# Moving VectorE's extra operations behind the last output of a gate/up unit

## The chip, the cores and the metric

The kernel runs on one core of one Trainium2 chip. A core has a matrix engine (TensorE, PE in the profile, with its weight loads as PEld), three elementwise engines (VectorE or DVE, ScalarE or ACT, GpSimd or POOL) and SyncE (SP), which issues most of the transfers. The engines run side by side, each through its own list of instructions in order, and wait for one another through semaphores. The metric is the device time of one execution in microseconds; lower is better.

## The reference

The inputs are in bfloat16: x of 2048 tokens by 1024, the attention weights, the gate, up and down weights (1024 x 3584 twice, 3584 x 1024 once), and a conditioning row c.

```python
mod = (silu(c) @ w_mod)                      # six rows of 1024: sa, ca, ga, sb, cb, gb
h = layernorm(x) * (1 + ca) + sa
x = x + ga * A(h)                            # 32 heads of linear attention, then @ wo
h = layernorm(x) * (1 + cb) + sb
x = x + gb * ((gelu(h @ w_gate) * (h @ w_up)) @ w_down)
```

The change touches the last line alone, and the scaling of h ahead of it.

## The kernel before, in words

**Stages.** From 0 to about 242 us the kernel does the modulation rows, the first layer norm, the attention and most of its output projection. From there to 605 us it does the gate and up products, and from 605 us to the end the down product with the last addition to x. TensorE's list has no barrier between stages.

**Gate/up units.** The 2048 tokens are two halves p of 1024. For each half the 3584 hidden columns are 14 pairs of 128, so there are 28 units v = 0 to 27 (`unit(v)`). A unit needs, for gate and up (t = 0 and 1), a 256 x 1024 by 1024 x 1024 product. It is done as a 2 x 2 x 2 block product with seven block products in place of eight, P1 to P7, each four matmuls deep over the contraction, so 8 matmuls with both t and 56 in a unit. They are run in the order 1, 5, 6, 2, 7, 3, 4. From 5 on but for 2, the two t alternate from matmul to matmul; in P1 and P2 t = 0 is done before t = 1. The seven products need sums of blocks as operands:

- `t_sum(v, k)` (L1438, VectorE, two operations of 128 x 512 each, tiles tp) makes the weight sums of unit v; k = 3 is a copy on ScalarE (L1427). There is one set of tp tiles, so the sums of unit v + 1 follow the product of unit v that last read the tile. P5 reads tp 0, P6 tp 1, P7 tp 2, P3 tp 3, P4 tp 4.
- `s_sum(p, i, j)` (L1418, 128 x 1024, tiles ss) makes the sums of the normalised tokens, once for each half. `ar_copy(p)` (L1404, ScalarE) copies a block of tokens into another type, as two operations.
- `mod2` (L754, VectorE) and `mod2_act` (L785, ScalarE) scale and shift the normalised tokens of the second half before that.

Results stand in eight PSUM banks, four pairs BA, BB, BC, BE (one of a pair for gate, one for up). P1 writes BA. `pcp` (L1470, ScalarE) copies BA to BB, for t = 0 and then 1; P6 adds to BB. P5 writes BE, `escp` (L1473, ScalarE) copies it to es. After P6 `padd` (L1476, VectorE) writes BB + es to BC, for both t, and P7 adds to BB after that; then `padd` writes BB + es to BE. P2, P7, P3 and P4 each end one of a unit's four outputs, in BA, BE, BC and BB: `gelu` (L1481, ScalarE) reads the gate bank, `y_out` (L1485, VectorE) multiplies with the up bank into yr. The last one, of P4 in BB, is put off: `held` keeps it until P1's first half of the next unit has been recorded, and then `y_store(v)` (L1493, SP) sends the unit's yr to scr_y. So pcp of a unit, which writes BB, waits for the y_out of the unit before.

**The order around it.** In these two stages nothing is planned by costs: the order of each engine's list is the order in which the Python code records operations. `unit` records each product and behind it the operations that belong to it, and then runs the hooks that were hung on it: `hook(v, k, fn)` runs fn behind product k of unit v, after that product's own work. So a hook on (v, 4) comes behind the unit's last product and ahead of the next unit's P1, and with it ahead of the held y_out; a hook on (v + 1, 1) comes behind that y_out, behind pcp and behind `t_sum(v + 1, 4)`. Before, the extra work of VectorE is hung in turn on (v, 7) and (v, 4): mod2 in units 5 and 6 (and 9), s_sum of the second half in units 10 to 13, and from unit 14 on the weight sums of the down stage.

**Down stage.** Step j takes 256 tokens and 1024 output columns over 28 blocks of hidden columns in 14 pairs k. It has the same seven products over most pairs (`dprod`, L1611): over pairs 0 to 12 in steps 1 to 7, over pairs 0 to 5 (NEA = 6) in step 0, where the other pairs are done plainly (`plain`). `raw_load(k)` (L1565, SP) loads the weights of a pair (tiles bx and wst), `b_sum(k, i)` makes their five derived operands (L1577 on VectorE; i = 3 is a copy on ScalarE, L1571), `y_load` (L1586, SP) fetches yl, and `a_sum(i, ..)` (L1605, VectorE) makes the sums of yl. `b_sums` yields four calls per pair, the last with i = 3 and 4 together. `ew` is that row for pairs 0 to 7, spent by hooks in units 14 to 27; `lw` is the rest, and `lws(n)` spends n calls of it. `dpcp` (L1644), `descp` (L1648) and `dpadd` (L1652, VectorE) do what pcp, escp and padd do above.

Of the kernel before, what the change touches and what calls it, by code (L numbers as in the profile page):

```python
# [346 lines left out]
def bass_adaLN_cond__linear_attn_block__geglu_ffn__prompt_kernel(  # L347
# [18 lines left out]
    with ExitStack() as es:  # L366
# [410 lines left out]
        def mod2(p, h, c0, n, dc0=0, dc1=NDC):  # L777
            mods(h2ap, r_h2p, (p, h), sc2, c0 * P, (c0 + n) * P, dc0, dc1, "h2")
# [620 lines left out]
        S32 = [[t_.ap().bitcast(f32) for t_ in r_] for r_ in SS]  # L1399
        T32 = [t_.ap().bitcast(f32) for t_ in TP]  # L1400

        def ar_copy(p):
            for k in (0, 2):
                sch.op(A, lambda e, k=k: e.activation(A22R[p][:, k:k + 2, :], H2[p][1][:, ND2 + k:ND2 + k + 2, :], ACTF.Copy),  # L1404
                       rd=r_h2(p, 1, ND2 + k, ND2 + k + 2), wr=r_ar(p, k, k + 2), note=f"arcp {p}.{k}")

# [16 lines left out]
        def t_sum(u, k):  # L1423
            if k == 3:
                ap, rd = wq(u, 1, 1)
                for t in range(2):
                    sch.op(A, lambda e, t=t: e.activation(TP[3][:, t, :, :], ap[:, t, :, :], ACTF.Copy), rd=rd[t:t + 1], wr=r_tp(3, t, t + 1), note=f"brcp u{u}")  # L1427
                return
            if k == 0:
                (in0, r0), (in1, r1) = wq(u, 0, 1), wq(u, 0, 0)  # L1430
            elif k == 1:
                (in0, r0), (in1, r1) = wq(u, 1, 1), (T32[0], r_tp(0))
            elif k == 2:
                (in0, r0), (in1, r1) = wq(u, 1, 1), wq(u, 0, 1)
            else:
                (in0, r0), (in1, r1) = wq(u, 1, 0), (T32[1], r_tp(1))
            for t in range(2):
                sch.op(V, lambda e, t=t: e.tensor_tensor(TP[k][:, t, :, :], in0[:, t, :, :], in1[:, t, :, :], ALU.subtract),  # L1438
                       rd=r0[t:t + 1] + (r1[t:t + 1] if len(r1) == 2 else [(r1[0][0] + t * 2048, r1[0][0] + (t + 1) * 2048, r1[0][2])]),
                       wr=r_tp(k, t, t + 1), note=f"tsum{k} u{u}")  # L1440
# [58 lines left out]
        def hook(v, k, fn):  # L1499
            HK.setdefault((v, k), []).append(fn)  # L1500

        def unit(v, order=(1, 5, 6, 2, 7, 3, 4)):
            more = v + 1 < 2 * NFP
            for k in order:
                if isinstance(k, tuple):
                    wo_chunk(*k)
                    continue
                if callable(k):
                    k()
                    continue  # L1510
                late = v == 0 and k == 2
                gb_, gk, yl, yh = (None, 1, 0, 0) if late else {2: (BA, 0, 0, 0), 7: (BE, 1, 1, 1), 3: (BC, 0, 1, 0), 4: (BB, 0, 0, 1)}.get(k, (None, 1, 0, 0))
                if k > 2:
                    for dc in range(ND2):
                        for t in range(2):
                            prod(v, t, k, [dc])
                for t in range(2):
                    if k < 3:
                        prod(v, t, k)
                    if k == 1:  # L1520
                        if held[0]:
                            held[0]()
                            held[0] = None
                            y_store(v - 1)
                        pcp(t)
                    elif k == 5:
                        escp(t)
                    elif k == 6:
                        padd(t, BC)
                    elif k == 7:  # L1530
                        padd(t, BE)
                    if gb_ is not None and t == gk:
                        gelu(gb_)
                        ig = (gi[0] - 1) % 2
                if k == 2 and v + 2 < 2 * NFP:
                    wt_dma(v + 2)
                if k == 4:
                    held[0] = lambda: y_out(ig, BB, v, 0, 1)
                elif gb_ is not None:
                    y_out(ig, gb_, v, yl, yh)  # L1540
                if k == 1:
                    if v == 0:
                        ar_copy(0)
                    else:
                        t_sum(v, 4)
                if more:
                    if k == (3 if v == 0 else 5):
                        t_sum(v + 1, 0)
                    if k == (3 if v == 0 else 2):
                        t_sum(v + 1, 1)  # L1550
                    if k == 3:
                        t_sum(v + 1, 3)
                        t_sum(v + 1, 2)
                for f_ in HK.pop((v, k), ()):
                    f_()

# [62 lines left out]
        def dprod(j, i, k0, k1, n=512):  # L1619
            t, ks = j % 2, range(k0, k1)  # L1620
            if i in (1, 2):
                lhs = [ya(i - 1, 0, k) for k in ks]
                rhs = [(BXT[k][:, i - 1, :], r_bx(k, i - 1, i)) for k in ks]
            else:
                xi, ti = {5: (0, 0), 6: (1, 1), 7: (0, 2), 3: (1, 3), 4: (2, 4)}[i]
                lhs = [(XS[xi][:, k, :], r_xq(xi, k, k + 1)) for k in ks]
                rhs = [(TT[k][ti][:, 0:n], r_bt(k, ti)) for k in ks]
            b = {1: BA, 2: BA, 5: BE, 6: BB, 7: BB, 4: BB, 3: BC}[i] + t
            dmm(b, i in (1, 5) and k0 == 0, lhs, rhs, f"down j{j} P{i}", 0, n)
# [83 lines left out]
        for i in range(4):  # L1713
            hook(i + 1, 2, lambda i=i: x1_store(i))
        for n in range(4):
            hook(5 + n // 2, (7, 4)[n % 2], lambda n=n: mod2(1, 0, 0, 4, 2 * n, 2 * n + 2))
        hook(9, 7, lambda: mod2(1, 1, 0, 4, 0, 3))
        hook(9, 4, lambda: mod2(1, 1, 0, 4, 3, 5))
        hook(9, 6, lambda: mod2_act(1, 1, 0, 4, 5, 6))
        hook(9, 3, lambda: mod2_act(1, 1, 0, 4, 6, 8))  # L1720
        hook(10, 3, lambda: ar_copy(1))
        for n in range(8):
            i, j = divmod(n, 2)
            hook(10 + n // 2, (7, 4)[n % 2], lambda i=i, j=j: s_sum(1, i, j))
        hook(12, 2, lambda: raw_load(0))
        hook(13, 2, lambda: raw_load(1))
        ew = b_sums(range(NEA + 2))
        for n in range(4 * NEA):
            v, k = 14 + n // 2, (7, 4)[n % 2]
            hook(v, k, lambda: next(ew)())  # L1730
            if n % 4 == 3 and 2 + n // 4 < NEA:
                hook(v, k, lambda n=n: raw_load(2 + n // 4))
# [3 lines left out]
        hook(24, 2, lambda: raw_load(6))  # L1736
        hook(26, 2, lambda: raw_load(7))
        hook(26, 7, lambda: next(ew)())
        hook(26, 4, lambda: next(ew)())
        V_ = 2 * NFP - 1  # L1740
        hook(V_, 5, lambda: a_sum(0, 0, NEA))
        hook(V_, 5, lambda: next(ew)())
# [14 lines left out]
        def lws(n):  # L1757
            for _ in range(n):
                next(lw)()
# [10 lines left out]
        dprod(0, 5, 0, NEA)  # L1770
        descp(0)
        a_sum(2, 0, NEA)
        lws(3)
        dprod(0, 6, 0, NEA)
        dpadd(0, BC)
        a_sum(3, 0, NEA)
        dprod(0, 2, 0, NEA)
        for l in range(2):
            y_load(1, l, 0, NEA)
# [1 line left out]
        dpadd(0, BE)  # L1781
        dprod(0, 3, 0, NEA)
        dprod(0, 4, 0, NEA)
        lws(6)
        for k in range(NEA, NKP):
            for s_ in range(2):
                for c in range(2):
# [148 lines left out]
```

## Time and profile before

| | us |
|---|---|
| median of three runs (790.52, 791.15, 792.69) | 791.15 |
| the profiled execution, its own time | 790.65 |
| its span, first to last instruction | 788.8 |
| TensorE busy in it | 775.3 |
| VectorE busy | 636.1 |
| ScalarE busy | 342.5 |
| clock granted to TensorE | 1.0 throughout |

A row of the timeline has start and length in us, engine, line, operation, tiles written and read, shapes and count; where the engine sat idle before it, the idle time and what ended it stand in brackets. In a list of waits the numbers are the total in us, how many times, and the longest. A row of the table of windows gives the window's length and then, for each engine, busy time and instructions. A unit starts where TensorE's rows turn to the tiles h20a (first half) or h21a (second half) and wt after a row with ar; unit 1 starts at 262.01, unit 14 at 428.18, the down stage at 605.01. A few matmul records are missing in the trace, so a group of eight can show as seven.

### The profile page before, as it was taken

The page shows a single profiled execution, that of the slowest core. Times are in us where ns is not written, and L with a number is a line of the kernel's source. Part 1 is how long each engine was busy: PE and PEld are TensorE (multiplying, and loading weights), DVE is VectorE, ACT ScalarE, POOL GpSimd, SP SyncE. Part 2 cuts the span into 40 slices and gives each one's busy share as a digit, 9 for nine tenths or more (in the row PEclk, how much of TensorE's full clock was granted, in tenths as well). Part 3 has the DMA queues.
Part 4 walks back from the last instruction along what each step waited for, and adds up shares of the span by engine and source line. Part 5 has one row for each costly group of instructions (what it writes and reads, how often), then busy time and mean ns, then how long its engine had stood idle before and what let it go on. Part 6 is the DMA issues. An engine that isn't in the chain of part 4 may idle for free. (4 is left out here: it accounts for less than half of the span.)

```text
span 788.8 us, 11024 instructions
## 1 busy us (share of the span) xinstructions
PE 775.3 (98%) x3840; PEld 495.6 (63%) x3904; DVE 636.1 (81%) x1078; ACT 342.5 (43%) x582; POOL 43.9 (6%) x126
## 2 busy tenths in 40 slices
PE   7999999999999999999999999999999999999998
PEld 4444445666445667777666767777776576666766
DVE  6799899983598877888999888898989786567664
ACT  2497743232583576675634444453545011111110
POOL 2131300000230001010000000000000000000000
PEclk9999999999999999999999999999999999999999
DMA  9789749836596378556355557555546354434340
GB/s 288 246 175 240 169 109 237 207 72 130 133 256 167 116 205 253 154 135 170 99 151 148 159 168 233 141 147 147 142 117 203 102 170 128 140 113 139 109 141 27
DMA packets 211407, 125.93 MB, mean 160 GB/s; under 512 B 70668, under 2 KB 201748, under 8 KB 211352
## 3 DMA queue, kind: packets, MB, share of 16 engines
q1 hardware_dynamic: 211336, 125.23, 58.5%
q8 instruction: 31, 0.51, 0.3%
q14 instruction: 24, 0.20, 0.1%
q10 hardware_dynamic: 16, 0.00, 0.0%
HBM read 88.35 MB, written 23.22 MB: 141 GB/s over the span
## 5 line engine op out<-in xcount | busy, mean ns | idle before, releaser
L1464 PE MATMUL ps_all<-ss,tp 128*128 128x512 f32 x896 | 226.2, 403 | 1.1 <-ACT ps_all L1470 0.6
L1464 PEld LDWEIGHTS ps_all<-ss,tp 128*128 128x128 f32 x896 | 167.7, 188 | 43.6 <-ACT ps_all L1470 2.2
L1481 ACT ACTIVATE ge<-ps_all 128x512 f32<-128x512 f32 x112 | 66.7, 596 | 134.7 <-DVE ps_all L1476 83.2
L1611 PE MATMUL ps_all<-bt,xs 128*128 128x512 f32 (+1 forms) x485 | 118.5, 399 | 0.9 <-DVE ps_all L1652 0.9
L1611 PEld LDWEIGHTS ps_all<-bt,xs 128*128 128x128 f32 x485 | 91.1, 188 | 22.3 <-DVE ps_all L1652 1.4
L1485 DVE TENSOR_TENSOR yr<-ge,ps_all 128x512 bf16<-128x512 f32 x112 | 76.7, 685 | 31.6 <-PE ps_all L1464 17.8
L1476 DVE TENSOR_TENSOR ps_all<-ps_all,es 128x512 f32<-128x512 f32 x112 | 72.4, 691 | 8.7 <-PE ps_all L1464 7.5
L1438 DVE TENSOR_TENSOR tp<-wt 128x512 fp32r<-128x512 bf16 x112 | 72.1, 684 | 1.3
L1438 DVE TENSOR_TENSOR tp<-wt,tp 128x512 fp32r<-128x512 bf16 x112 | 72.0, 683 | 0.0
L1611 PE MATMUL ps_all<-bx,yl 128*128 128x512 bf16 (+2 forms) x269 | 59.8, 360 | 0.7
L965 PE MATMUL ps_all<-h1T,wq 128*128 128x512 bf16 x256 | 56.7, 379 | 0.0
L914 PE MATMUL ps_all<-wk,h1T 128*128 128x512 bf16 x239 | 55.3, 379 | 1.1 <-DMA wk<-in_A_wqkv_dram 0.5
L1299 PE MATMUL ps_all<-w,pq 128*128 128x512 bf16 x251 | 55.9, 379 | 0.4
L1644 ACT ACTIVATE ps_all<-ps_all 128x512 f32<-128x512 f32 x8 | 4.7, 582 | 117.4 <-PE ps_all L1611 117.4
L1464 PE MATMUL ps_all<-ar,tp 128*128 128x512 f32 x224 | 55.3, 389 | 0.0
L903 ACT ACTIVATE eb<-ps_all 128x512 f32<-128x512 f32 x64 | 36.4, 593 | 37.1 <-PE ps_all L914 15.4
L1464 PE MATMUL ps_all<-h21a,wt 128*128 128x512 bf16 x210 | 50.1, 380 | 1.0
L1464 PE MATMUL ps_all<-h20a,wt 128*128 128x512 bf16 x210 | 50.0, 380 | 0.9
L1464 PEld LDWEIGHTS ps_all<-ar,tp 128*128 128x128 f32 x224 | 42.1, 188 | 8.7
L1470 ACT ACTIVATE ps_all<-ps_all 128x512 f32<-128x512 f32 x56 | 32.6, 582 | 30.6 <-DVE yr L1485 15.4
L965 PEld LDWEIGHTS ps_all<-h1T,wq 128*128 128x128 bf16 x256 | 25.0, 98 | 30.0
L1299 PEld LDWEIGHTS ps_all<-w,pq 128*128 128x128 bf16 x256 | 24.7, 98 | 30.3 <-issue 0.5
(146 smaller groups left out, 903.8 us busy)
## 6 DMA issues: line engine op xcount, KB each, us to landing
wt<-in_B_w_gate_dram SPq DMA_DIRECT2D x28, 512.0 KB, 4.0
wt<-in_B_w_up_dram SPq DMA_DIRECT2D x28, 512.0 KB, 5.2
scr_y<-yr SPq DMA_DIRECT2D x56, 256.0 KB, 2.9
yl<-scr_y SPq DMA_DIRECT2D x12, 832.0 KB, 4.3
wmst<-in_w_mod_dram SPq DMA_DIRECT2D x6, 1024.0 KB, 5.7
wmq<-in_w_mod_dram SPq DMA_DIRECT2D x8, 512.0 KB, 6.1
rb<-scr_rd SPq DMA_DIRECT2D x32, 128.0 KB, 2.9
scr_x<-xall SPq DMA_DIRECT2D x4, 1024.0 KB, 7.1
```

What stands on the lines that cost most here:

```text
L903: sch.op(A, lambda e: e.activation(EB[i][:, :], PS(bank), ACTF.Exp), prd=pr(bank), wr=rng, note=f"{note}.exp")
L914: o = sch.op(T, lambda e, dc=dc: e.matmul(PS(bank), H1[sg][:, ci, dc, :], W_[:, dc, jg * 512:(jg + 1) * 512], start=(dc == 0), stop=(dc == ...
L965: o = sch.op(T, lambda e, dc=dc: e.matmul(PS(b), WQ[:, dc, qc * P:(qc + 1) * P], H1[sg][:, :, dc, :], start=(dc == 0), stop=(dc == NDC - 1 ...
L1299: last[half] = sch.op(T, lambda e, g=g, half=half: e.matmul(PS(b0 + half), PQ[sg][:, g, ci * P:(ci + 1) * P], W2[:, g, half * 512:(half + ...
L1438: sch.op(V, lambda e, t=t: e.tensor_tensor(TP[k][:, t, :, :], in0[:, t, :, :], in1[:, t, :, :], ALU.subtract), rd=r0[t:t + 1] + (r1[t:t + ...
L1464: o = sch.op(T, lambda e, l_=l_, r_=r_, dc=dc: e.matmul(PS(b), l_, r_, start=fresh and dc == 0, stop=dc == ND2 - 1, skip_group_check=True) ...
L1470: sch.op(A, lambda e: e.activation(PS(BB + t), PS(BA + t), ACTF.Copy), prd=pr(BA + t), pwr=pr(BB + t), note="pcp")
L1476: sch.op(V, lambda e: e.tensor_tensor(PS(dst + t), PS(BB + t), ES[t][:, :], ALU.add), prd=pr(BB + t), rd=r_2k(OFF_ES[t], f"es{t}"), pwr=pr ...
L1481: sch.op(A, lambda e: e.activation(GE[i][:, :], PS(b), ACTF.Gelu_apprx_tanh), prd=pr(b), wr=r_2k(OFF_GE[i], f"ge{i}"), note="gelu")
L1485: sch.op(V, lambda e: e.tensor_tensor(YR[:, 2 * (v % 2) + l, h * SGW:(h + 1) * SGW], GE[i][:, :], PS(b + 1), ALU.mult), rd=r_2k(OFF_GE[i], ...
L1611: pend_ = sch.op(T, lambda e, l_=l_, r_=r_, i=i: e.matmul(PS(b, c0, c1), l_, r_, start=fresh and i == 0, stop=i == n - 1, skip_group_check ...
L1644: sch.op(A, lambda e: e.activation(PS(BB + t), PS(BA + t), ACTF.Copy), prd=pr(BA + t), pwr=pr(BB + t), note="pcp")
```

## The change

TensorE's list is the same in both. The changes are in what is hung where:

- mod2, s_sum of the second half and the early weight sums that hung on (v, 4) hang on (v + 1, 1). The loads of raw weights that hung with them move along, on SP behind the y stores of unit v, and the b_sum copies on ScalarE (L1571) come behind pcp.
- `t_sum(1, 1)` and `t_sum(1, 2)` are recorded behind P1 of unit 1, behind the held y_out of unit 0, and no more behind P3 of unit 0.
- `ar_copy(1)`, two copies behind P3 of unit 10, becomes one behind P6 of unit 10 and one behind P6 of unit 11.
- In step 0 of the down stage three calls of lws ahead of the first `dpadd` become one behind it and behind `a_sum(3)`; the six later ones become eight.

```diff
-        def ar_copy(p):
-            for k in (0, 2):
+        def ar_copy(p, ks=(0, 2)):
+            for k in ks:
...
                     else:
+                        if v == 1:
+                            t_sum(1, 1)
+                            t_sum(1, 2)
                         t_sum(v, 4)
                 if more:
                     if k == (3 if v == 0 else 5):
                         t_sum(v + 1, 0)
-                    if k == (3 if v == 0 else 2):
+                    if k == 2 and v:
                         t_sum(v + 1, 1)
                     if k == 3:
                         t_sum(v + 1, 3)
-                        t_sum(v + 1, 2)
+                        if v:
+                            t_sum(v + 1, 2)
...
         for n in range(4):
-            hook(5 + n // 2, (7, 4)[n % 2], lambda n=n: mod2(1, 0, 0, 4, 2 * n, 2 * n + 2))
+            hook(5 + (n + 1) // 2, (7, 1)[n % 2], lambda n=n: mod2(1, 0, 0, 4, 2 * n, 2 * n + 2))
...
-        hook(9, 4, lambda: mod2(1, 1, 0, 4, 3, 5))
+        hook(10, 1, lambda: mod2(1, 1, 0, 4, 3, 5))
...
-        hook(10, 3, lambda: ar_copy(1))
+        hook(10, 6, lambda: ar_copy(1, (0,)))
+        hook(11, 6, lambda: ar_copy(1, (2,)))
         for n in range(8):
             i, j = divmod(n, 2)
-            hook(10 + n // 2, (7, 4)[n % 2], lambda i=i, j=j: s_sum(1, i, j))
+            hook(10 + (n + 1) // 2, (7, 1)[n % 2], lambda i=i, j=j: s_sum(1, i, j))
...
         for n in range(4 * NEA):
-            v, k = 14 + n // 2, (7, 4)[n % 2]
+            v, k = 14 + (n + 1) // 2, (7, 1)[n % 2]
             hook(v, k, lambda: next(ew)())
...
-        hook(26, 4, lambda: next(ew)())
+        hook(27, 1, lambda: next(ew)())
...
         a_sum(2, 0, NEA)
-        lws(3)
         dprod(0, 6, 0, NEA)
         dpadd(0, BC)
         a_sum(3, 0, NEA)
+        lws(1)
         dprod(0, 2, 0, NEA)
...
-        lws(6)
+        lws(8)
```

## The prediction

> **What bounds the kernel now.** I read the page first (busy shares, the chain that ended last), then the lists of waits, then a table of windows cut at unit starts, then the timelines around the windows that stood out. TensorE is busy almost without a break, and 44% of the chain is its own:
>
> ```profile
> PE 775.3 (98%) x3840; PEld 495.6 (63%) x3904; DVE 636.1 (81%) x1078; ACT 342.5 (43%) x582; POOL 43.9 (6%) x126
> ```
>
> So a change that leaves TensorE's instructions alone can only gain what TensorE waits. The lists of waits name three places, first that of TensorE's matmuls, then that of all engines:
>
> ```profile
> PE ps_all L1611 <- DVE ps_all L1652: 0.9, 1, 0.9
> PE ps_all L1464 <- ACT ps_all L1470: 0.6, 1, 0.6
> ```
>
> ```profile
> ACT ps_all L1470 <- DVE yr L1485: 15.4, 17, 1.8
> ...
> PEld ps_all L1464 <- ACT ps_all L1470: 2.8, 6, 0.6
> ```
>
> In one place TensorE waits for an addition (L1652); in the others, matmul or weight load, for the copy pcp (L1470), and 17 of pcp's own waits were for y_out (L1485). The windows say how much and in which units:
>
> ```profile
> 262.01:275.45 13.44, 12.78 (x56) 8.85 (x57) 11.64 (x20) 7.05 (x14) 0.92 (x3) 1.00 0.51 151
> 275.45:288.07 12.62, 12.55 (x57) 8.90 (x57) 10.04 (x17) 8.66 (x17) 1.12 (x5) 1.00 0.77 228
> 376.48:389.08 12.60, 12.53 (x56) 8.93 (x57) 11.51 (x20) 6.97 (x13) 0.00 (x0) 1.00 0.46 126
> 428.18:441.21 13.03, 12.82 (x56) 8.85 (x57) 12.15 (x20) 5.59 (x10) 0.00 (x0) 1.00 0.48 134
> 441.21:453.81 12.60, 12.53 (x56) 8.92 (x57) 11.18 (x19) 5.68 (x10) 0.00 (x0) 1.00 0.52 146
> ```
>
> The first number after each window is its length. Most units take 12.60 us; unit 1 (the first row) takes 13.44, and units 11 to 14 (the fourth row is unit 14) take 13.03, 13.04, 13.03, 13.03. Unit 14's timeline shows the wait itself:
>
> ```profile
> 429.73 4.44 PE L1464 MATMUL ps_all<-ss,tp 128*128 128x512 f32 x16
> 429.74 1.22 DVE L1418 TENSOR_TENSOR ss<-h21a,ss 128x1024 fp32r<-128x1024 bf16 x1
> 430.88 0.68 DVE L1485 TENSOR_TENSOR yr<-ge,ps_all 128x512 bf16<-128x512 f32 x1
> ...
> 431.65 0.58 ACT L1470 ACTIVATE ps_all<-ps_all 128x512 f32<-128x512 f32 x1 [1.81 <-DVE yr L1485]
> ...
> 432.28 1.46 PEld L1464 LDWEIGHTS ps_all<-ss,tp 128*128 128x128 f32 x7 [0.56 <-ACT ps_all L1470]
> 432.68 1.28 DVE L1438 TENSOR_TENSOR tp<-wt 128x512 fp32r<-128x512 bf16 x2
> ...
> 434.05 1.30 DVE L1476 TENSOR_TENSOR ps_all<-ps_all,es 128x512 f32<-128x512 f32 x2
> ```
>
> The unit before left its last product in bank BB+1. Its gelu (428.23, 0.60) was over at 428.83, but s_sum (L1418) stood ahead of y_out on VectorE; pcp into BB+1 waits for y_out, and P6's second matmul waits for pcp. In the down stage's start, three weight sums (L1577) stand ahead of the addition (L1652):
>
> ```profile
> 608.79 0.68 DVE L1577 TENSOR_TENSOR bt<-wst,bx 128x512 fp32r<-128x512 bf16 x1
> 609.50 0.69 DVE L1577 TENSOR_TENSOR bt<-wst,bt 128x512 fp32r<-128x512 bf16 x1
> 610.11 0.68 DVE L1577 TENSOR_TENSOR bt<-wst 128x512 fp32r<-128x512 bf16 x1
> 610.72 0.69 DVE L1652 TENSOR_TENSOR ps_all<-ps_all,es 128x512 f32<-128x512 f32 x1
> ...
> 611.46 4.40 PE L1611 MATMUL ps_all<-bt,xs 128*128 128x512 f32 x18 [0.90 <-DVE ps_all L1652]
> ```
>
> **The change, part by part.** TensorE's order of instructions stays as it was; VectorE, ScalarE and SP run the same work in another order (one row of two 128x1024 copies on ScalarE becomes two).
>
> *s_sum behind y_out (units 11 to 14).* y_out can start when the t_sum before it is issued (starts on VectorE lie 0.60 apart for a 0.68 us operation, 1.14 for s_sum): 428.54 + 1.20 = 429.74 instead of 430.88. pcp then ends near 431.1, before P6 wants the bank (near 431.75). The bubble of 13.03 - 12.60 = 0.43 goes. What is late next is the addition padd (L1476) ahead of P7, since VectorE has the same work before it: 429.74 y_out, 430.34 t_sum(v,4), 431.55 s_sum, 432.69 t_sum(v+1,0), 433.89 and 434.50 the two padds, the last over at 435.19. P7 began at 435.56 and its second matmul, the one that needs the second padd, 0.42 later (the pair takes 0.81, one takes 0.39); without the bubble that is 435.55. Add 0.05 for the handover (611.41 to 611.46 in the down rows): 0.31 to spare. Gain 0.43 + 0.44 + 0.43 + 0.43 = 1.73. Bounds: 0, if the bubble turns up elsewhere in these units, and 4 x 0.56 = 2.24 by the weight load's idle time; I take the windows, since they hold whole units.
>
> A rule of the Trainium skill ("VectorE: DVE Perf Modes", section "The DRAIN you can't avoid") speaks against this: it says that the next operation can't issue before the pipe of the one before is empty, with no overlap; laid end to end the operations above would make P7 late. The trace disagrees, with starts 0.60 apart under 0.68 us operations, so the sum stays at 1.73; by the page it would be 0.33 (the first rival has the working).
>
> *t_sum(1,1) and t_sum(1,2) behind unit 0's last y_out.* Before, they held y_out from 262.66 to 265.07 and pcp until 265.84. Now y_out goes as soon as its gelu is over (262.06 + 0.60), near 262.70; the sums follow at 263.30 and 264.51, the first over by 264.6, with P6 at 265.4. The bubble is 13.44 - 12.62 = 0.82. VectorE's row of work is as long: t_sum(1,4) 265.72, t_sum(2,0) 266.92, padds 268.12 and 268.73, over at 269.42, plus 0.05 is 269.47; P7's second matmul without the bubble is 269.80 + 0.42 - 0.82 = 269.40. That costs 0.07, so the gain is 0.75 (bounds 0 and 0.98, the longest idle of a weight load there).
>
> *lws(3), lws(6) become lws(1), lws(8).* After a_sum(2) (607.91, 0.96) the addition now waits only for P6's end, about 609.25; it runs about 609.35 to 610.05. In a unit P7 starts 1.33 after the first of P2's seven recorded matmuls; here five are recorded from 609.32, 0.43 less, so P7 could start at 610.22. It started at 611.46, 1.24 later, and its first pair takes 0.73 against 0.81, which gives 0.08 back: gain 1.16. a_sum(3) follows to 610.9, the one weight sum to 611.5, the second addition starts when P7 ends (613.15 - 1.16 = 611.99) without delay, and eight weight sums run to 617.7 where six ran to 617.5. The next consumers are the second pair's P5 at 632.14 - 1.16, with VectorE idle 2.13 before 628.05: 0.2 us late there costs nothing; were that idle gone, it would cost 0.2. Bounds 0.90 (the idle shown) and 1.4 (the weight load's wait for L1652 in the same list).
>
> *Edits put at nothing.* mod2 in units 6 and 7 no longer fills the 0.76 us in which VectorE waits for a gelu there: y_out 328.24 as now, t_sum 328.84, mod2 330.04 (0.65), t_sum 330.69, padds 331.90 and 332.50, over at 333.20 + 0.05, against P7's second matmul at 332.94 + 0.42 = 333.36. The cover is 0.11; gone, each unit pays what is over. Unit 10's mod2 moves the same way, but its padd had 0.30 idle. Twelve units with a weight sum (L1577, 0.68) or its last pair behind y_out: they run 12.60 now, no gain; padd there comes 0.45 after VectorE is free (597.85), and without that cover each would pay up to 0.60. Six copies on ScalarE (L1571, 0.62) go behind pcp: pcp starts 594.82, the copy 595.31 to 595.93, escp at 595.96 as before. ar_copy's halves (1.0 each) stand in the 1.83 idle before a gelu (382.95). On SP four pairs of weight loads (256 KB, 3.7 to 5.4 to land) go behind two y stores (0.6 each to issue) and are read two units, some 25 us, later; the stores go earlier, and the next pair of gate/up weights waits for P2, 4 us on. Lost cover there would show as t_sum waiting for a transfer.
>
> Sum: 1.73 + 0.75 + 1.16 = 3.64. The profiled execution took 790.65 (span 788.8, 1.85 around it), so 787.0. The median, 791.15, lies 0.5 above; the other runs are 790.52 and 792.69. I forecast the middle of 787.0 and 791.15 - 3.64 = 787.5: 787.3.
>
> **The rivals.**
> 1. *The bubble moves to P7.* Were VectorE's operations to run end to end, unit 14 would have y_out from 429.82, then 0.68 + 1.37 + 1.22 + 1.37 + 1.39 = 435.85, plus 0.05, against 435.55: 0.35 late in each of four units, 1.4 less, 788.7. The Trainium skill's rule on the pipe, above, amounts to this. Against it: every row shows the overlap. Chance 0.09.
> 2. *The bank stays the limit.* The same gap in four units running may mean that there are too few banks, whatever the order: then the 1.73 stays and 789.0 results. Against it: the product was ready for y_out at 428.83 and was read at 430.88, so the queue held the bank. The Trainium skill ("Perfetto Trace Analysis", section "Optimization Strategy") has it as a rule that consistent bubbles can mean too little PSUM; the trace does not bear it out here. Chance 0.04.
> 3. *Nothing reaches the end*, since later waits take it all: 790.8. After the bubbles TensorE runs unit after unit at 12.60, which speaks against it. Chance 0.05.
> 4. *Slower: padd comes late in the units with weight sums.* VectorE's extra 0.60 now stands between y_out and t_sum(v+1,0), directly ahead of padd. If all of it reached TensorE in 13 units, that is 7.8 - 3.6 = 4.2 more, 795.0. It passes the bound from 0.46 per unit on ((3.64 + 2.4) / 13). For it: 11.99 of 12.60 busy in unit 27. Against it: the 0.45 idle at padd, and the same work before padd as now. Chance 0.07.
>
> That the change does not do what it says is no rival: in the new list of VectorE every y_out named here stands directly behind the t_sum before it.
>
> **How the numbers follow.** All three bubbles going has chance 0.75. About 0.3%, 2.4 us, is what a measurement of this kernel can tell from no change, so 788.8 is the border. Faster: 0.72 of the 0.75, and 0.04 of the first rival; slower: the fourth, 0.07; same: the rest, 0.17. The range: from below, the upper bounds 2.24 + 0.98 + 1.4 give 790.65 - 4.6 = 786.05, taken as 786.2; from above, rivals 1 and 2 with 0.5 for the scatter, 789.5. That leaves out rivals 3 and 4 and a few tails, under 0.2.
>
> **What would show it.** Right: units 1 and 11 to 14 at 12.6 to 12.7 in the windows, no wait of a weight load for L1470 in them, y_out starting right behind t_sum, the addition L1652 starting near 609.4 less the earlier gains and P7 about 0.9 behind P2's start. Wrong: units 6 and 7 over 12.62, a wait of TensorE for L1476, units 15 to 27 over 12.60, or the second pair's P5 waiting for L1577 or L1605.

## The result and the profile after

The changed kernel takes 787.51 us (median of four runs, 787.04 to 788.23) against 791.07 (median of four, 790.52 to 792.69); the ratio is 0.9952, with a 95% interval of 0.9935 to 0.9970, so it is faster by about 0.5%. The forecast was 787.3. The profiled execution took 787.11 with a span of 785.2; the forecast for such a run was 787.0.

In the changed file the lines behind `unit` stand four lower than before: the down stage's products are L1615, its additions L1656, its pcp L1648, its weight sums L1581 on VectorE, its token sums L1609. The lines of a gate/up unit keep their numbers.

The page's list of busy times and the list of waits, after:

```profile
PE 778.4 (99%) x3904; PEld 495.8 (63%) x3904; DVE 635.6 (81%) x1078; ACT 343.6 (44%) x582; POOL 44.4 (6%) x126
```

```profile
ACT ps_all L1470 <- DVE yr L1485: 2.7, 4, 0.7
PEld ps_all L1464 <- ACT ps_all L1470: 0.6, 2, 0.3
PEld ps_all L1464 <- DVE ps_all L1476: 0.3, 1, 0.3
```

The same work is done in less time; that PE shows 64 instructions more is a matter of missing records, since TensorE's list is the same. pcp's waits for y_out fell from 17 with 15.4 us to 4 with 2.7, and the two weight loads that still wait for pcp lie in unit 0. TensorE's matmuls wait for no addition of the down stage any more. One weight load now waits for the addition padd (L1476), which is in unit 1.

The table of windows after, cut at the starts of units 1, 2, 11, 14 and 15 (length of the window, then busy time and instructions of PE, PEld, DVE, ACT, POOL, granted clock, DMA share, GB/s):

```profile
262.03:274.82 12.79, 12.79 (x57) 8.84 (x56) 11.78 (x21) 7.33 (x14) 1.24 (x4) 1.00 0.56 166
274.82:287.41 12.59, 12.59 (x57) 8.92 (x57) 9.84 (x17) 8.51 (x15) 1.01 (x4) 1.00 0.75 223
388.38:400.99 12.61, 12.61 (x58) 8.93 (x57) 12.08 (x19) 6.62 (x11) 0.00 (x0) 1.00 0.44 125
426.19:438.79 12.60, 12.60 (x58) 8.93 (x57) 12.07 (x20) 5.68 (x10) 0.00 (x0) 1.00 0.48 137
438.79:451.39 12.60, 12.60 (x58) 8.92 (x57) 11.18 (x19) 5.68 (x10) 0.00 (x0) 1.00 0.45 125
```

Units 11 to 14 went from 13.03 to 12.60, unit 1 from 13.44 to 12.79. From the down stage's first weight load to the first one from wst, at the start of the plain part, it takes 9.75, where it took 10.92. Unit 14's timeline shows the order that does it:

```profile
427.74 4.00 PE L1464 MATMUL ps_all<-ss,tp 128*128 128x512 f32 x16
427.75 0.68 DVE L1485 TENSOR_TENSOR yr<-ge,ps_all 128x512 bf16<-128x512 f32 x1
428.34 1.28 DVE L1438 TENSOR_TENSOR tp<-wt,tp 128x512 fp32r<-128x512 bf16 x2
428.52 0.58 ACT L1470 ACTIVATE ps_all<-ps_all 128x512 f32<-128x512 f32 x1 [0.68 <-DVE yr L1485]
...
429.55 1.22 DVE L1418 TENSOR_TENSOR ss<-h21a,ss 128x1024 fp32r<-128x1024 bf16 x1
...
431.89 1.28 DVE L1476 TENSOR_TENSOR ps_all<-ps_all,es 128x512 f32<-128x512 f32 x2
```

y_out starts 0.01 after P5 and P6 begin; before, it started 1.15 after. pcp still waits for it (0.68), but is over at 429.10, before P6 wants the bank. s_sum stands behind, and padd (431.89) comes in time. In the down stage's start:

```profile
606.66 1.47 PE L1615 MATMUL ps_all<-bx,yl 128*128 128x512 bf16 x6
606.93 0.70 DVE L1656 TENSOR_TENSOR ps_all<-ps_all,es 128x512 f32<-128x512 f32 x1 [0.49 <-PE ps_all L1615]
607.54 0.95 DVE L1609 TENSOR_TENSOR xs<-yl,xs 128x768 fp32r<-128x768 bf16 x1
607.78 4.48 PE L1615 MATMUL ps_all<-bt,xs 128*128 128x512 f32 x18
...
609.56 0.70 DVE L1656 TENSOR_TENSOR ps_all<-ps_all,es 128x512 f32<-128x512 f32 x1 [0.47 <-PE ps_all L1615]
```

The addition now waits for TensorE (0.49), and TensorE no more for the addition.

Where the time went, from the first weight loads of the units in both traces: unit 1 gave 0.65, units 2 to 10 together 0.07 (where no edit touches them they scatter between 12.59 and 12.67 from run to run), units 11 to 14 gave 1.73, the rest from the down stage's start 1.18, and unit 1 began 0.02 later; together that is the 3.60 by which the span fell.

### The profile page after: what moved, and what is told of

Read it like the earlier page. It is cut to its first block, busy times and chain, and to the rows that moved or that the text cites. A ratio compares the mean times of both kernels' runs of the same rounds, so it can differ in the third digit from the quotient of the medians.

```text
span 785.2 us, 11090 instructions
## 1 busy us (share of the span) xinstructions
PE 778.4 (99%) x3904; PEld 495.8 (63%) x3904; DVE 635.6 (81%) x1078; ACT 343.6 (44%) x582; POOL 44.4 (6%) x126
## 4 chain that ended last, share of the span: by engine, by line
PE 95%; DMA 2%; SPq 2%; DVE 0%; issue 0%; ACT 0%; DVEq 0%
PE ps_all L1464 45%; PE ps_all L1615 23%; PE ps_all L1299 7%; PE ps_all L965 7%; PE ps_all L929 6%; PE ps_all L914 6%; DMA mtb<-mb 1%; SPq L627 1%; DMA wmq<-in_w_mod_dram 1%; SPq L632 1%; PE ps_all L947 0%; PE ps_all L1230 0%; PE ps_all L1257 0%; SPq L621 0%; PE ps_all L874 0%
## 5 line engine op out<-in xcount | busy, mean ns | idle before, releaser
L1615 PE MATMUL ps_all<-bt,xs 128*128 128x512 f32 (+1 forms) x485 | 118.6, 399 | 0.0
L1615 PEld LDWEIGHTS ps_all<-bt,xs 128*128 128x128 f32 x485 | 91.2, 188 | 21.1
L1476 DVE TENSOR_TENSOR ps_all<-ps_all,es 128x512 f32<-128x512 f32 x112 | 72.2, 690 | 7.9 <-PE ps_all L1464 7.4
L1615 PE MATMUL ps_all<-bx,yl 128*128 128x512 bf16 (+1 forms) x282 | 61.2, 361 | 0.0
L1648 ACT ACTIVATE ps_all<-ps_all 128x512 f32<-128x512 f32 x8 | 4.7, 582 | 117.4 <-PE ps_all L1615 117.4
L1464 PE MATMUL ps_all<-h21a,wt 128*128 128x512 bf16 x224 | 53.2, 380 | 0.0
L1464 PE MATMUL ps_all<-h20a,wt 128*128 128x512 bf16 x224 | 53.0, 380 | 0.0
L1615 PEld LDWEIGHTS ps_all<-bx,yl 128*128 128x128 bf16 x282 | 24.4, 98 | 30.5 <-issue 4.4
```

Source lines behind the costliest of these rows:

```text
L1464: o = sch.op(T, lambda e, l_=l_, r_=r_, dc=dc: e.matmul(PS(b), l_, r_, start=fresh and dc == 0, stop=dc == ND2 - 1, skip_group_check=True) ...
L1476: sch.op(V, lambda e: e.tensor_tensor(PS(dst + t), PS(BB + t), ES[t][:, :], ALU.add), prd=pr(BB + t), rd=r_2k(OFF_ES[t], f"es{t}"), pwr=pr ...
L1615: pend_ = sch.op(T, lambda e, l_=l_, r_=r_, i=i: e.matmul(PS(b, c0, c1), l_, r_, start=fresh and i == 0, stop=i == n - 1, skip_group_check ...
```

## The experiments

All start from the changed kernel but the tenth. Where unit 1 begins varies from run to run between 261.76 and 263.66 with no edit there, so single times scatter by 2 us, and I read each run by the lengths of its units and of the stretch in the down stage (first weight load to the first one from wst, at the start of the plain part). In this table units 3 to 10 and 15 to 27 are left out; they take 12.59 to 12.67 and 12.60 but for the two runs named below the table.

| run | own time | unit 1 | unit 2 | 11 | 12 | 13 | 14 | down |
|---|---|---|---|---|---|---|---|---|
| before | 790.65 | 13.44 | 12.61 | 13.03 | 13.03 | 13.03 | 13.03 | 10.92 |
| after | 787.11 | 12.79 | 12.59 | 12.60 | 12.60 | 12.60 | 12.60 | 9.75 |
| 1 s_sum back | 790.56 | 12.79 | 12.60 | 13.03 | 13.09 | 13.01 | 13.09 | 9.75 |
| 2 unit 1's sums back | 788.73 | 13.44 | 12.62 | 12.60 | 12.60 | 12.60 | 12.60 | 9.75 |
| 3 down stage back | 789.12 | 12.84 | 12.62 | 12.60 | 12.60 | 12.60 | 12.60 | 10.92 |
| 4 all the rest back | 787.27 | 12.79 | 12.59 | 13.10 | 12.60 | 12.60 | 12.60 | 9.75 |
| 5 less room | 789.88 | 12.80 | 12.60 | 12.85 | 12.59 | 12.87 | 12.60 | 9.75 |
| 6 no room | 797.52 | 12.79 | 12.60 | 13.13 | 12.83 | 12.93 | 12.81 | 9.75 |
| 7 t_sum(1,4) later | 788.76 | 12.69 | 12.92 | 12.60 | 12.60 | 12.60 | 12.60 | 9.75 |
| 8 two sums moved | 792.33 | 16.39 | 13.78 | 12.60 | 12.60 | 12.60 | 12.60 | 9.75 |
| 9 ar_copy back | 787.78 | 12.79 | 12.59 | 13.13 | 12.60 | 12.60 | 12.60 | 9.75 |
| 10 before, ar_copy spread | 790.48 | 13.45 | 12.60 | 13.03 | 13.03 | 13.03 | 13.03 | 10.90 |
| 11 two sums, right order | 787.43 | 12.60 | 13.11 | 12.60 | 12.60 | 12.60 | 12.60 | 9.75 |
| 12 sum behind y_out | 787.05 | 12.60 | 12.73 | 12.60 | 12.60 | 12.60 | 12.60 | 9.75 |

In run 5 units 15 to 26 change between about 12.77 and 12.62, and 27 takes 13.26; in run 6 units 15 to 26 take 13.19 to 13.59, most of them 13.22, and 27 takes 13.70.

### 1. s_sum ahead of y_out again

```diff
-            hook(10 + (n + 1) // 2, (7, 1)[n % 2], lambda i=i, j=j: s_sum(1, i, j))
+            hook(10 + n // 2, (7, 4)[n % 2], lambda i=i, j=j: s_sum(1, i, j))
```

> The changed kernel with only the four later s_sum hung on the unit's last product again, ahead of y_out. Theory (the place in VectorE's list holds the bank): units 11 to 14 go back from 12.60 to 13.03 us each, 1.72 in all, the weight load there waits for L1470 again, and nothing else moves. Rival (the other parts of the change freed the queue or the banks, and the bubble would be gone anyway): units 11 to 14 stay at 12.60.

Units 11 to 14 are longer by 0.43, 0.49, 0.41 and 0.49, 1.82 in all, and nothing else moved. The list of waits has the weight loads waiting for pcp again:

```profile
ACT ps_all L1470 <- DVE yr L1485: 7.2, 4, 1.8
PEld ps_all L1464 <- ACT ps_all L1470: 2.8, 6, 0.6
```

So the term for s_sum is shown in place and size.

### 2. The first pair's sums ahead of unit 0's last y_out again

```diff
-                        if v == 1:
-                            t_sum(1, 1)
-                            t_sum(1, 2)
                         t_sum(v, 4)
...
-                    if k == 2 and v:
+                    if k == (3 if v == 0 else 2):
                         t_sum(v + 1, 1)
...
-                        if v:
-                            t_sum(v + 1, 2)
+                        t_sum(v + 1, 2)
```

> The changed kernel with only t_sum(1, 1) and t_sum(1, 2) ahead of unit 0's last y_out again. Theory: unit 1 goes from 12.79 to 13.44 us, 0.65 more, no other unit moves. Rival (a later wait takes the time back): unit 1 is longer, but units 2 to 9 are shorter by as much.

Unit 1 takes 13.44, as before the change, 0.65 more; no other unit moved.

### 3. The down stage's weight sums ahead of the addition again

```diff
+        lws(3)
         dprod(0, 6, 0, NEA)
         dpadd(0, BC)
         a_sum(3, 0, NEA)
-        lws(1)
...
-        lws(8)
+        lws(6)
```

> The changed kernel with only lws(3) ahead of the first addition of the down stage again, and lws(6). Theory: P7 of step 0 starts 1.2 us later after the stage's start, and all behind it, 1.17 us in all. Rival (the two weight sums moved back relieve the stretch before step 1): less than 0.9, since VectorE has 0.2 us less to do before step 1's sums.

The stretch takes 10.92 again, 1.17 more, and the units are as in the changed kernel but for 0.05 in unit 1. TensorE's wait is the one of before:

```profile
607.81 1.24 PE L1615 MATMUL ps_all<-bx,yl 128*128 128x512 bf16 x5
609.95 2.81 PE L1615 MATMUL ps_all<-bt,xs 128*128 128x512 f32 x11 [0.90 <-DVE ps_all L1656]
```

### 4, 9 and 10. The edits put at nothing

Run 4 puts back mod2, ar_copy and the weight sums of the twelve units together; run 9 ar_copy alone; run 10 makes the edit to ar_copy alone in the kernel before.

```diff
-            hook(5 + (n + 1) // 2, (7, 1)[n % 2], lambda n=n: mod2(1, 0, 0, 4, 2 * n, 2 * n + 2))
+            hook(5 + n // 2, (7, 4)[n % 2], lambda n=n: mod2(1, 0, 0, 4, 2 * n, 2 * n + 2))
...
-        hook(10, 1, lambda: mod2(1, 1, 0, 4, 3, 5))
+        hook(9, 4, lambda: mod2(1, 1, 0, 4, 3, 5))
...
-        hook(10, 6, lambda: ar_copy(1, (0,)))
-        hook(11, 6, lambda: ar_copy(1, (2,)))
+        hook(10, 3, lambda: ar_copy(1))
...
-            v, k = 14 + (n + 1) // 2, (7, 1)[n % 2]
+            v, k = 14 + n // 2, (7, 4)[n % 2]
...
-        hook(27, 1, lambda: next(ew)())
+        hook(26, 4, lambda: next(ew)())
```

> The changed kernel with mod2, ar_copy, the early weight sums, their loads and their copies where they were before. Theory: no unit moves, 6 and 7 and 15 to 27 included: 0.0 within 0.1 over the units and the down stage. Rival (these twenty moves gave part of the gain, or took some): unit lengths differ by more than 0.05 in those units.

No unit was to move, and unit 11 took 13.10. The timeline of run 4's ScalarE suggested the two copies of ar_copy, so run 9 tested them alone:

```diff
-        hook(10, 6, lambda: ar_copy(1, (0,)))
-        hook(11, 6, lambda: ar_copy(1, (2,)))
+        hook(10, 3, lambda: ar_copy(1))
```

> The changed kernel with only ar_copy(1) behind P3 of unit 10 again, in one piece. Theory (two copies of 1.0 on ScalarE hold the gelu of unit 10's last output, and so y_out): unit 11 at 13.10 us, 0.50 more, as in the run that put all the rest back; no other unit moves. Rival (mod2 of unit 10 or the weight sums did it): unit 11 at 12.60.

Unit 11 took 13.13, 0.53 more, and everything else stayed: ar_copy is the cause, and mod2 and the twelve units' weight sums are worth nothing, as predicted. Run 9's timeline at the start of unit 11 (388.60):

```profile
388.36 1.99 ACT L1404 ACTIVATE ar<-h21b 128x1024 fp32r<-128x1024 bf16 x2
390.25 0.58 ACT L1481 ACTIVATE ge<-ps_all 128x512 f32<-128x512 f32 x1
...
390.87 0.69 DVE L1485 TENSOR_TENSOR yr<-ge,ps_all 128x512 bf16<-128x512 f32 x1 [0.62 <-ACT ge L1481]
...
395.76 0.19 PEld L1464 LDWEIGHTS ps_all<-ss,tp 128*128 128x128 f32 x1 [0.35 <-DVE ps_all L1476]
396.36 1.69 PEld L1464 LDWEIGHTS ps_all<-ss,tp 128*128 128x128 f32 x8 [0.41 <-DVE ps_all L1476]
```

The copies stand ahead of the gelu of unit 10's last product on ScalarE. y_out starts 2.27 into the unit; in the changed kernel it started 1.57 into it (389.95). All that follows on VectorE is late by that, s_sum included, and so is padd: the weight loads of P7 wait for it twice. Run 10:

```diff
-        def ar_copy(p):
-            for k in (0, 2):
+        def ar_copy(p, ks=(0, 2)):
+            for k in ks:
...
-        hook(10, 3, lambda: ar_copy(1))
+        hook(10, 6, lambda: ar_copy(1, (0,)))
+        hook(11, 6, lambda: ar_copy(1, (2,)))
```

> The kernel before with only ar_copy(1) split and moved behind P6 of units 10 and 11. Theory (in unit 11 s_sum and the copies held the same y_out side by side, so that taking one away alone gives nothing): units 11 to 14 at 13.03 as before, 0.0 gained. Rival (each is worth its own part): unit 11 down by 0.4 to 0.5.

Alone, the spread copies give nothing: unit 11 is 13.03 with and without. Unit 11 had two holds side by side. In the kernel before, that unit's held gelu and y_out stand so:

```profile
388.83 1.99 ACT L1404 ACTIVATE ar<-h21b 128x1024 fp32r<-128x1024 bf16 x2
390.73 0.59 ACT L1481 ACTIVATE ge<-ps_all 128x512 f32<-128x512 f32 x1
```

```profile
390.64 1.22 DVE L1418 TENSOR_TENSOR ss<-h21b 128x1024 fp32r<-128x1024 bf16 x1
391.77 0.68 DVE L1485 TENSOR_TENSOR yr<-ge,ps_all 128x512 bf16<-128x512 f32 x1
```

The gelu was over at 391.32 and s_sum let y_out go at 391.77: s_sum was the later of the two and hid the other. Taking away one alone gives nothing here (run 9: 13.13, run 10: 13.03); taking away both gives 12.60.

### 5 and 6. How near VectorE's row of work is to the limit

Both record more work on VectorE behind t_sum(v, 4), with the sums' own values written again: half an operation in units 11 to 14 and two from unit 15 on in run 5, one and three in run 6.

```diff
+        def t_again(u, n, half=False):
+            (in0, r0), r1 = wq(u, 1, 0), r_tp(1)
+            for t in [1] * n:
+                d = ND2 // 2 if half else ND2
+                sch.op(V, lambda e, t=t: e.tensor_tensor(TP[4][:, t, 0:d, :], in0[:, t, 0:d, :], T32[1][:, t, 0:d, :], ALU.subtract),
...
                         t_sum(v, 4)
+                        if 11 <= v <= 14:
+                            t_again(v, 1, True)
+                        elif v > 14:
+                            t_again(v, 2)
```

(Run 6 has `t_again(v, 1)` and `t_again(v, 3)`. In these two files the unit's lines stand eight lower: products L1472, padd L1484.)

> The changed kernel with work added to VectorE directly behind t_sum(v, 4): the second operation of t_sum(v, 4) done again on half its columns in units 11 to 14 (0.33 from start to start), and wholly, twice, in units 15 to 27 (1.20). The result stays the same. First theory, as in the prediction (what is late is P7's second matmul, 0.31 to spare): units 11 to 14 at 12.62. Second theory (the wait for padd sits on the weight load, which runs some 0.23 ahead of its matmul; 0.09 is spare to its slot and 0.12 more is free): 0.33 - 0.21 = 0.12, units 11 to 14 at 12.72. Both: units 15 to 27 at 12.60, since 0.6 is idle ahead of padd there and P7 has more. Rival 4 of the prediction (extra work there reaches TensorE): 13 x 1.2 more.

> As the run with less room, but the whole operation in units 11 to 14 (0.60) and three of it in units 15 to 27 (1.80). First theory: 0.60 - 0.31 = 0.29, units 11 to 14 at 12.89; units 15 to 26 at 13.02. Second theory: 0.60 - 0.21 = 0.39, units 11 to 14 at 12.99; units 15 to 26 at 13.13. Rival 2 of the prediction (banks, not the queue): no change from more work behind y_out, 12.60.

The lists of waits show what became the limit, first run 5's, then run 6's:

```profile
PEld ps_all L1472 <- DVE ps_all L1484: 4.5, 15, 0.4
```

```profile
PEld ps_all L1472 <- DVE ps_all L1484: 14.7, 33, 0.8
```

An added operation writes the tile that the one before it wrote, and then it starts 0.71 after that one, not 0.60; so the half operation added 0.455 to the row (0.71 and then 0.34 to the next start, less the 0.60 of before), not 0.34. Units 11 to 14 missed what was expected too: neither theory had long and short units by turns (12.85, 12.59, 12.87, 12.60 in run 5 where 12.62 or 12.72 was expected; 13.13, 12.83, 12.93, 12.81 in run 6 where 12.89 or 12.99 was), though the second theory is near their averages, 12.73 and 12.92. Unit 11 of run 5 shows the rule for the wait at P7:

```profile
395.05 1.29 DVE L1484 TENSOR_TENSOR ps_all<-ps_all,es 128x512 f32<-128x512 f32 x2
```

```profile
395.81 0.19 PEld L1472 LDWEIGHTS ps_all<-ss,tp 128*128 128x128 f32 x1
396.39 1.69 PEld L1472 LDWEIGHTS ps_all<-ss,tp 128*128 128x128 f32 x8 [0.39 <-DVE ps_all L1484]
```

The second padd is over at 396.335, and what follows it at once is not the matmul but its weight load, at 396.388, where the load's slot was 396.023 (0.216 behind the load before it). The load is 0.365 late and the unit 0.25 longer, so 0.12 of a load's lateness is free: the next load follows it 0.109 later, where it follows 0.231 later when nothing is late. In unit 1 of the changed kernel the load is 0.309 late (269.474 against 269.165), which makes 0.19, and that is what the unit is over 12.60.

The held y_outs of units 11 and 12 in run 5 show why long and short units take turns:

```profile
390.45 0.68 DVE L1493 TENSOR_TENSOR yr<-ge,ps_all 128x512 bf16<-128x512 f32 x1
403.05 0.68 DVE L1493 TENSOR_TENSOR yr<-ge,ps_all 128x512 bf16<-128x512 f32 x1
```

They are 12.60 apart, though unit 11 takes 12.85: the wait at P7 makes TensorE's unit longer and leaves VectorE's row where it was. So y_out comes 1.57 into unit 11 and 1.31 into unit 12, whose load is only 0.11 late, which is free; VectorE then waits for P2 again (0.24), and unit 13 is late in full (0.37).

Units 15 to 26 missed what was expected in both runs: about 0.10 on average in run 5, by turns as above, where nothing was expected, and 0.62 in most units of run 6 where 0.53 or 0.42 was. VectorE's windows of run 6, unit 11 and a unit with weight sums (columns as above):

```profile
388.51:401.64 13.13, 12.96 (x56) 8.83 (x56) 13.01 (x20) 6.63 (x11) 0.00 (x0) 1.00 0.43 120
506.72:519.94 13.22, 13.06 (x56) 8.84 (x56) 13.03 (x22) 6.22 (x11) 0.00 (x0) 1.00 0.56 159
```

VectorE is busy 13.0 of 13.1 and 13.2. There the length of a unit is no more TensorE's 12.60 and a delay, but VectorE's own row, carried from unit to unit; my expectations had counted each unit by itself.

### 7, 8, 11 and 12. The 0.19 in unit 1

Ahead of its additions unit 1 has four weight sums on VectorE, eight operations, where other units have two, and the weight load that needs its second padd comes 0.31 late. Run 7 records t_sum(1,4), which P4 needs last, behind P6's additions:

```diff
-                        t_sum(v, 4)
+                        if v > 1:
+                            t_sum(v, 4)
+                if k == 6 and v == 1:
+                    t_sum(1, 4)
```

> The changed kernel with t_sum(1, 4) of unit 1 behind the two padds that follow P6, in place of ahead of them; it is read only by P4, at the unit's end. Theory: what is left of unit 1's bubble is padd coming late behind five sums; without one of them unit 1 falls from 12.79 to 12.61, 0.18 us, and nothing else moves; in the time 0.18 of 787 can't be told from no change. Rival (the rest is a switch between operand types or a transfer): 12.79 stays.

Unit 1 fell to 12.69 only, and unit 2 rose to 12.92: together 25.61 against 25.38. The sum pushed back unit 1's y_outs, second additions and gelus, and so the held y_out and pcp of unit 2. Run 8 records t_sum(1,4) one product later, behind P2's output, and t_sum(2,1) behind P7's output:

```diff
-                        t_sum(v, 4)
+                        if v > 1:
+                            t_sum(v, 4)
...
-                    if k == 2 and v:
+                    if v == 1 and k == 2:
+                        t_sum(1, 4)
+                    if v and k == (7 if v == 1 else 2):
                         t_sum(v + 1, 1)
```

> The changed kernel with t_sum(1, 4) of unit 1 behind the output of P2 (not directly behind the padds) and t_sum(2, 1) in exchange behind the output of P7, where VectorE waits 0.9 for a gelu. Theory (the run with t_sum(1, 4) behind the padds cost unit 2 its 0.3 because the second pair of padds, and with it the gelus, came 1.2 later): units 1 and 2 both at 12.60 to 12.63, 0.18 us less than the changed kernel in them. Rival (unit 2 pays for anything that leaves its place in unit 1): unit 2 over 12.7 again.

This edit was ill made. At that place the transfer of unit 3's weights into unit 1's tile has been recorded already, so t_sum(1,4) waits for the transfer and P4 of unit 1 takes an operand made with a block of unit 3's weights in place of unit 1's. The run took 792.38 (median of ten; 1.0016 of before, interval 1.0006 to 1.0026). TensorE's timeline:

```profile
269.83 3.58 PE L1464 MATMUL ps_all<-ss,tp 128*128 128x512 f32 x15
276.06 3.00 PE L1464 MATMUL ps_all<-ar,tp 128*128 128x512 f32 x8 [2.65 <-DVE ps_all L1476]
```

It says nothing on unit 1's 0.19, but shows what a wait for a transfer costs in VectorE's row (2.48 and 0.97 in its timeline): 4.8 us over both units, with a spell of half clock that the last section shows. Run 11 joins run 7's place for t_sum(1,4) with run 8's for t_sum(2,1):

```diff
+                        if v > 1:
+                            t_sum(v, 4)
+                if k == 6 and v == 1:
+                    t_sum(1, 4)
...
-                    if k == 2 and v:
+                    if v and k == (7 if v == 1 else 2):
                         t_sum(v + 1, 1)
```

> From the changed kernel, t_sum(1,4) goes from behind P1 to behind P6's two additions in unit 1, still ahead of the load of unit 3's weights, and t_sum(2,1) from behind P2's output to behind P7's output of unit 1. Theory (unit 1 is 0.19 long because four weight sums stand ahead of its second padd, and the weight load that needs it comes 0.31 after its slot): two operations less ahead of the padds bring them 1.2 us forward, and with t_sum(2,1) out of the way the second padds and the gelus of unit 1 come no later than before, so both unit 1 and unit 2 take 12.60 to 12.63 (12.79 and 12.59 in the changed kernel, 12.69 and 12.92 with the first move alone, 16.39 and 13.78 where the sum had to wait for a transfer). That is 0.17 us less than the changed kernel, about 787.3, less than times can tell; no wait of a weight load for pcp over 0.3, granted clock 1.00 throughout. Rival (VectorE has no room for five weight sums in unit 1 whatever their order): unit 1 and 2 together stay at 25.38 or more.

Unit 1 is at 12.60 as the theory had it, unit 2 at 13.11, and together 25.71: the rival's number, but not for its reason. VectorE had 1.24 to spare before the held y_out; ScalarE was late, and ScalarE waited for GpSimd. The timeline of GpSimd and of ScalarE, run 11:

```profile
273.49 0.73 POOL L703 TENSOR_SCALAR ve<-st 128x1 f32<-128x1 f32 x1 [5.51 <-ACT xl L701]
274.30 0.57 POOL L704 TENSOR_TENSOR rs<-ve,neghalf 128x1 f32<-128x1 f32 x1
274.95 0.47 POOL L706 TENSOR_TENSOR nm<-mv,rs 128x1 f32<-128x1 f32 x1
```

```profile
275.45 1.24 ACT L689 ACTIVATE xl<-xall,nm,rs 128x1024 bf16<-128x1024 bf16 x1 [0.59 <-POOL nm L706]
276.60 0.58 ACT L1481 ACTIVATE ge<-ps_all 128x512 f32<-128x512 f32 x1
```

L703 and L706, layer-norm statistics of 128 values, took 0.73 and 0.47 where they take 0.19 in the changed kernel, and each ended 0.05 after an operation of t_sum on VectorE. Run 8, with t_sum(2,1) in the same place, has the same two rows at 0.73 and 0.47, each 0.05 behind a t_sum, so they are no chance of one run. The pass L689 waits for them, and the gelu ahead of the held y_out waits for L689. Run 12 puts t_sum(2,1) behind unit 1's third y_out instead:

```diff
-                    if v and k == (7 if v == 1 else 2):
+                    if v and k == (3 if v == 1 else 2):
                         t_sum(v + 1, 1)
```

> As the kernel before this one (unit 1 12.60, unit 2 13.11), but t_sum(2,1) is recorded behind unit 1's third output y_out(BC), ahead of t_sum(2,3). There GpSimd's L703 and L706, which ran 0.73 and 0.47 instead of 0.19 and each ended 0.05 after an operation of t_sum(2,1) or t_sum(2,2), held ScalarE's pass L689, and it held the gelu ahead of the held y_out. Theory (GpSimd can't run beside a VectorE operation that reads two SBUF operands): VectorE is idle or in y_out while L703 and L706 run, so L703 takes 0.19 again and L689 starts near 274.75 after a unit start of 274.53 (275.45 there). y_out then waits for t_sum(2,1) and t_sum(2,2) on VectorE and not for the gelu, starts near 276.86 (277.21 there), pcp ends near 278.2, its weight load is 0.2 late past its slot, and unit 2 takes about 12.70; unit 1 12.60; both together 25.30 against 25.71. Rival (the stretched GpSimd rows are chance or profiling, and the four weight sums between the outputs of unit 1 and the held y_out are what costs): L703 and L706 stay as long, or fall without effect, and unit 2 stays at 13.0 or more.

```profile
273.75 0.19 POOL L703 TENSOR_SCALAR ve<-st 128x1 f32<-128x1 f32 x1 [5.50 <-ACT xl L701]
274.03 0.57 POOL L704 TENSOR_TENSOR rs<-ve,neghalf 128x1 f32<-128x1 f32 x1
274.68 0.19 POOL L706 TENSOR_TENSOR nm<-mv,rs 128x1 f32<-128x1 f32 x1
```

Both are at 0.19 again, L689 starts 0.22 after unit 2 begins (0.92 in run 11), and unit 2 takes 12.73, where 12.70 was expected. What holds y_out now is VectorE's own row, as expected. Units 1 and 2 take 25.33 together, 0.05 less than in the changed kernel. The time is 787.28 (median of four), 0.9945 of before with an interval of 0.9928 to 0.9961: not to be told apart from the change itself. Unit 1's 0.19 can be moved, but of these placements none keeps more than 0.05 of it.

## Why the prediction was right

- *s_sum behind y_out, 1.73.* Measured 1.73 (1.82 when undone). The mechanism is as stated: y_out behind t_sum, pcp over before P6, padd in time. Two things in that step were not right. The 0.31 to spare was counted to P7's second matmul, but the wait sits on that matmul's weight load, and 0.12 of lateness is free there; by the second padd's end (433.174 in unit 14) and that load's start (433.318) the spare, with 0.05 for the handover, is 0.09 and 0.12, together 0.21. And unit 11's share was not s_sum's alone.
- *ar_copy at nothing.* This is the step that failed, and that the sum came out right all the same is luck: the change moved the copies as well. Adding the edit alone does give nothing (run 10), but 0.50 to 0.53 of unit 11 depend on it (runs 4 and 9). Looking only for what the moved copies might cost, I had not asked what they held where they stood: before, the gelu in unit 11 ended at 391.32, not shortly after the unit began as in unit 14, whose rows I had carried over to all four.
- *t_sum(1,1) and t_sum(1,2), 0.75.* Measured 0.65. The mechanism was right, the lateness was mis-sized: I had 0.07, by the matmul, and it was 0.19, by the weight load. The additions came as worked out (the second over at 269.42 as forecast).
- *lws, 1.16.* Measured 1.17 (to 1.18 up to the end). The addition started at 606.93; 609.4 less the 2.43 gained by then is 606.97. VectorE's idle before the second pair's P5, 2.13 before, is 0.93 now, so the cover held.
- *mod2, weight sums in twelve units, copies on ScalarE, SP.* Nothing, as put: runs 4 and 9 together leave no unit but 11 changed. My sign for failure, units 6 and 7 over 12.62, was too narrow: they took 12.64 and 12.63, but 12.63 and 12.63 in run 4, where mod2 is back. It came out at nothing by a small margin: with mod2 behind y_out the weight load that waits for the second padd is 0.09 and 0.11 late in these units (not late in run 4), and 0.12 is free.
- *Rival 1, the bubble moves to P7.* Not in units 11 to 14. The starts are still 0.60 apart under operations of 0.68. The rule of the Trainium skill behind it ("VectorE: DVE Perf Modes", section "The DRAIN you can't avoid") was seen here only for an operation that writes or reads what the one before it wrote: 0.71 apart in runs 5 and 6, and in the kernel before from 608.79 to 609.50, two rows that the prediction shows. The same section goes on to say that a next operation that is not held starts earlier, which the prediction left out; so the Trainium skill need not stand against the 0.60. The bubble did move to P7 in small in unit 1 (0.19), where VectorE has more to do.
- *Rival 2, the bank stays the limit.* The bubble went with the same eight banks, and came back with the order alone (run 1).
- *Rival 3, nothing reaches the end.* The whole 3.60 did: no later unit is longer, and from the down stage's start on the time is shorter by the 1.17 of its first stretch and not longer elsewhere.
- *Rival 4, padd late in the units with weight sums.* Units 15 to 27 stayed at 12.60. Runs 5 and 6 show how near it was: two more operations in each of these units cost about 0.10, and three 0.62.

## What to carry to other kernels

In an in-order queue, work that nobody awaits belongs behind the operation that frees a buffer, and what decides whether it may stand there is the next awaited operation, checked down to TensorE's weight load and not to its matmul. Before an edit is put at nothing, ask on which engine the moved work held something, and whether another hold hides that one: two holds on one operation show their price only when both are gone. When VectorE's free time in a unit is used up, count its row over several units, since lateness is then carried on.

## What the runs showed of the hardware

- *The wait is on the weight load.* At P7 a weight load runs about 0.23 ahead of its matmul, and the wait for the bank that the matmul adds to holds the load. It may be 0.12 late at no cost, since the next load then follows after 0.11 and not after 0.23; beyond that all of it counts (0.31 late cost 0.19, 0.365 late cost 0.25; 0.11 late in unit 12 of run 5 cost nothing).
- *Small GpSimd operations stood still beside VectorE.* Operations of 0.19 took 0.73 and 0.47 (runs 8 and 11) and ended 0.05 after a VectorE operation with two operands in SBUF; begun beside y_out, which has one in PSUM, L706 took 0.19 (run 12). The Trainium skill ("SBUF — State Buffer", section "Who interferes with whom") says that a VectorE instruction with two SBUF inputs contends with a GpSimd instruction that reads SBUF; runs 11 and 12 agree with it. The cost in run 11, 0.82 us on GpSimd, reached TensorE by way of ScalarE's queue, a gelu, y_out and pcp.
- *The clock fell after a short stall.* In run 8 TensorE stood idle for 2.65 us up to 276.06, and the granted clock was 0.5 from 277.81 to 281.23, 3.41 us, in which the matmuls ran 0.43 apart and not 0.23. The table of windows of that run, columns as above:

```profile
270.00:273.40 3.40, 3.40 (x15) 2.46 (x14) 0.92 (x2) 0.00 (x0) 0.00 (x0) 1.00 0.97 270
273.40:276.10 2.70, 0.05 (x2) 0.04 (x1) 1.73 (x4) 0.06 (x1) 0.00 (x0) 1.00 1.08 382
276.10:277.90 1.80, 1.70 (x6) 1.21 (x7) 1.70 (x3) 1.80 (x4) 0.00 (x0) 0.98 0.22 83
277.90:278.10 0.20, 0.20 (x2) 0.10 (x2) 0.20 (x2) 0.20 (x1) 0.18 (x1) 0.50 0.00 0
278.10:281.40 3.30, 3.30 (x10) 1.23 (x9) 2.29 (x4) 2.71 (x5) 1.58 (x3) 0.53 0.00 0
```

The clock was still 1.0 when TensorE began again, and fell 1.75 later; unit 2, which holds 2.38 of the 3.41, took 13.78. Two of the run's ten executions have a mean clock of 1.000 to three digits, which leaves no room for such a stretch, so it did not come every time; how long TensorE stood in those is not on record. The Trainium skill ("TensorE: Matmul & The Clock Gate", section "What's actually happening") gives about 3.4 us of idle time as what lowers the clock; here 2.65 came before it, and the length of the slow stretch, 3.41, is the length that the Trainium skill gives there for the window. The kernel before lost 1.2 in one place of the down stage at a clock of 1.0 throughout.
